# Gate terms copied raw and scaled once a batch, running totals on TensorE, z columns a step later, one subtraction a step

## The chip, the cores and the metric

The kernel runs on one core of a Trainium2 chip. Its engines run their own instruction queues in order, each queue waiting on counters of the others: TensorE (PE; its weight loads are PEld), VectorE (DVE), ScalarE (ACT), GpSimd (POOL) and SyncE (SP, which issues DMAs). The metric is the device time of one execution in microseconds; the median over several runs counts.

## The reference

The work is a linear attention, a mixture of experts on its result, and a SoLU block:

```
proj = q or k @ w_phi (64 -> 128);  proj -= max|proj|;  phi = [exp(proj), exp(-proj)]
kv = phi(k)^T v;  z = sum over tokens of phi(k)
x = (phi(q) kv) / (phi(q) z + 1e-6)                       # 8 batches x 8 heads x 576 tokens
logits = x @ w_gate + bias[modality];  expert = first argmax;  gate = softmax at it
y = gate * relu(x @ w1[expert]) @ w2[expert]              # 4608 tokens, 512 wide, 8 experts
h = y @ w_in;  solu = h * softmax(h);  out = layernorm(solu) * g_ln @ w_out
```

## The kernel before, in words

**Attention.** Eight units (a pair of batches times a half of the heads) of nine steps each make 72 steps, numbered 0 to 71. A step projects one tile of k and one of q into a PSUM tile `pj` (128x1024), from which VectorE takes the largest magnitude (`m`, L191) and subtracts it (L196, once for k into `xsk`, once for q into `xsq`). ScalarE takes the two exponentials of k (`e`, L203 and L204). Two steps later (LAGF) TensorE transposes `xsq` into a PSUM tile `tp`, of which ScalarE makes the exponentials of q (`qp`, L263), and it adds `e` into `kv` (L209); GpSimd adds `e` into `es` (L248, L224 for the remainder tiles), the sums over tokens. After the fifth and the ninth step of a unit its half is finished: ScalarE copies `kv` out (`kt`, L251), TensorE makes from it the features-to-output matrix `kf` with the gate weights folded in (L330), and, in the step after, the z columns of it from `es` by 16 matmuls of one column (`z_part`, L310 with `es`; the trace counts each twice).

**Tokens.** A token tile is 16 matmuls of `qp` by `kf` (L310, again 32 in the trace) into a `tp` tile of 73 columns a head: 64 output columns, 8 gate terms, one denominator. VectorE makes the reciprocal `r` of the denominator (L409, L410), multiplies the gate terms by it (L411, `gs`, 128x32) and the output by it (L415, `xt`, 128x256). At most two items, z columns and token tiles together, run in a step (COLS), so steps hold none, one or two token tiles; per unit there is one group of two two-token steps and a one-token step, and one group of two two-token steps. The tiles `tp` share three PSUM buffers among the transposes, `kf`, z, tokens and gating.

**Gating.** After a batch's four or five token tiles of both head halves (nine gatings in all), VectorE sums the gate terms over the heads (L427), adds the bias, finds the first largest and a one-hot `oh`. Two bf16 matmuls give the rank of a token among those of its expert in a tile and the tile's totals (L449, L450); ScalarE copies them to `g_rk` (L455), VectorE adds the totals up tile by tile in `base` (L468, L470, one small addition a tile) and computes each token's row (L475 and after), and GpSimd scatters the rows by indirect DMA (L482). From the totals, VectorE makes a table (`early.pick`, L694 to L706) by which the first chunk of expert weights is loaded, and ScalarE and VectorE split it into two parts (L776, L777) at step 63 + STEP0.

**After that** come the experts and the SoLU block, to the end of the span: float32 products made of three fp32r matmuls each. The change does not touch them.

**Order.** TensorE runs in the order in which the code is written. VectorE, ScalarE and GpSimd are put in order by a planner at build time, so an instruction's place follows from the planner's times, and a queue's head blocks all behind it.

Of the kernel before, what the change touches and what calls it, by code (L numbers as in the profile page):

```python
# [16 lines left out]
P = 128  # L17
# [3 lines left out]
E = 8  # L21
# [27 lines left out]
STEP0 = 6  # L49
# [68 lines left out]
def attention(ctx, tc, c, cnt, xe, q, qr, k, kr, v, ld, early, m, late):  # L118
# [60 lines left out]
    def project(u, jobs):  # L179
# [12 lines left out]
        return [(nm, i, features(pj[:, :, a], m[:, :, a], nm)) for a, (nm, i) in enumerate(jobs)]  # L192

    def features(pj, m, kind):
        x = w3p.tile([P, 4, F], F32, name="xs" + kind, bufs=4 if kind == "q" else 3)
        V.tensor_tensor(  # L196
            out=x.rearrange("p (j r) f -> p r j f", r=2), in0=pj,
            in1=m.unsqueeze(3).broadcast_to([P, 2, 2, F]), op=ALU.subtract,
        )
        if kind == "q":  # L200
            return x
# [134 lines left out]
    def finish_kv(u, half):  # L336
# [3 lines left out]
        after.append(Item("64", lambda: z_part(u, half), ready=lambda: step[0] > at))  # L340
# [43 lines left out]
    def tokens(u, i):  # L384
# [3 lines left out]
        if u.g == 0:  # L388
            if a == 0:
                w = 1 if part == 2 else 4  # L390
                t = xp.tile([P, w, ROW], F32, name=f"xt{w}")
# [6 lines left out]
            if i in (0, 4):  # L398
                gs[grp] = gp.tile([P, 5, H, E], F32, name="gs")
# [8 lines left out]
        r = gp.tile([P, 4], F32, name="r", bufs=3)  # L408
        V.tensor_scalar(out=r, in0=tp[:, :, D + E], scalar1=1e-6, scalar2=None, op0=ALU.add)  # L409
        V.reciprocal(r, r)  # L410
        V.tensor_tensor(  # L411
            out=gs[grp][:, i - 4 * grp, 4 * u.g : 4 * u.g + 4, :],
            in0=tp[:, :, D : D + E], in1=r.unsqueeze(2).broadcast_to([P, 4, E]), op=ALU.mult,
        )
# [5 lines left out]
    def gating(u, first, n, pace=0, counted=None):  # L420
# [3 lines left out]
        gt = gs[0][:, 0:n] if first == 0 else gs[1][:, first - 4 : first - 4 + n]  # L424
# [22 lines left out]
        rkp = tps.tile([P, 2, n, E], F32, name="tp")  # L447
        ohf = oh.rearrange("p t e -> p (t e)")
        T.matmul(rkp[:, 0].rearrange("p t e -> p (t e)"), lhsT=c.tri_bf, rhs=ohf, start=True, stop=True, skip_group_check=True)  # L449
        T.matmul(rkp[:, 1].rearrange("p t e -> p (t e)"), lhsT=c.ones_bf, rhs=ohf, start=False, stop=True, skip_group_check=True)  # L450
        rk = w("rk", [P, 2, 5, E])[:, :, :n, :]
        if tiles[0] == 7:
            V.tensor_copy(rk, rkp)
        else:
            A.copy(rk, rkp)  # L455
# [11 lines left out]
        base = w("base", [P, 6, E])  # L467
        V.tensor_copy(base[:, 0, :], cnt[0])  # L468
        for a in range(n):
# [1074 lines left out]
```

## Time and profile before

| | us |
|---|---|
| median of 3 runs | 1204.37 (1201.35 to 1208.66) |
| profiled execution: its time / its span | 1209.89 / 1207.7 |
| PE busy | 1166.4 (97 %) |
| DVE busy | 842.5 (70 %) |
| ACT busy | 576.9 (48 %) |
| POOL busy | 404.1 (33 %) |
| mean granted TensorE clock | 0.985 of full |

Attention ends at about 345 us of the span, and the experts and the SoLU block fill the rest. POOL is at six to eight tenths in attention and far below after. A share of busy time says little here: what counts is where PE, the engine that is nearly always busy, stands still, and at which clock it works after. Matmul ends are modelled, so a busy PE isn't PE at its peak.

### The profile page before, as it was taken

The page shows a single profiled execution, that of the slowest core. Times are in us where ns is not written, and L with a number is a line of the kernel's source. Part 1 is how long each engine was busy: PE and PEld are TensorE (multiplying, and loading weights), DVE is VectorE, ACT ScalarE, POOL GpSimd, SP SyncE. Part 2 cuts the span into 40 slices and gives each one's busy share as a digit, 9 for nine tenths or more (in the row PEclk, how much of TensorE's full clock was granted, in tenths as well). Part 3 has the DMA queues.
Part 4 walks back from the last instruction along what each step waited for, and adds up shares of the span by engine and source line. Part 5 has one row for each costly group of instructions (what it writes and reads, how often), then busy time and mean ns, then how long its engine had stood idle before and what let it go on. Part 6 is the DMA issues. An engine that isn't in the chain of part 4 may idle for free.

```text
span 1207.7 us, 27753 instructions
## 1 busy us (share of the span) xinstructions
PE 1166.4 (97%) x10658; PEld 1017.8 (84%) x10658; DVE 842.5 (70%) x1606; ACT 576.9 (48%) x974; POOL 404.1 (33%) x460
## 2 busy tenths in 40 slices
PE   7998999997989999999999999999999999999997
PEld 5787887886879999999999999977777778888885
DVE  6689889798666577787777877665655565566561
ACT  6455554655443455555555654643434343444342
POOL 4967867866640000000000000123233333433331
PEclk9899999999899999999999999999999999999999
DMA  9523433332231322145231324787877856556541
GB/s 322 181 80 123 137 95 120 123 122 80 86 111 62 83 86 71 53 133 166 57 85 54 88 67 129 200 206 206 226 202 202 224 136 149 147 134 151 148 119 48
DMA packets 249657, 157.40 MB, mean 130 GB/s; under 512 B 168752, under 2 KB 227376, under 8 KB 249520
## 3 DMA queue, kind: packets, MB, share of 16 engines
q1 hardware_dynamic: 243472, 136.39, 41.4%
q0 software_dynamic: 5760, 19.03, 4.1%
q8 instruction: 86, 1.41, 0.5%
q14 instruction: 51, 0.42, 0.1%
q10 hardware_dynamic: 288, 0.16, 0.0%
HBM read 167.12 MB, written 51.37 MB: 181 GB/s over the span
## 4 chain that ended last, share of the span: by engine, by line
PE 41%; DMA 6%; issue 1%; ACT 1%; DVE 1%; SPq 1%; POOLq 0%; ACTq 0%; DVEq 0%
PE tp L932 20%; PE h L932 19%; DMA turned<-whi 2%; DMA wlo<-turned 2%; DMA gd<-xe 1%; PE tp L1251 1%; SPq L1102 1%; DMA ldk<-in_moe_w_dram 1%; PE tp L747 0%; DMA gt<-gd 0%; DMA yd<-yo 0%; PE tp L1235 0%; DMA out_dram<-wab,gt 0%; ACT ex L1121 0%; ACT whi L1153 0%
## 5 line engine op out<-in xcount | busy, mean ns | idle before, releaser
L777 POOL TENSOR_TENSOR yTl<-yin,yTh 128x512 fp32r<-128x512 f32 x36 | 47.4, 1317 | 415.4 <-PE tp L932 403.1
L248 POOL TENSOR_TENSOR es<-es,e 128x512 f32<-128x512 f32 x128 | 162.1, 1273 | 50.6 <-ACT e L204 43.4
L932 PE MATMUL tp<-xTh,whi 128*128 128x256 f32 x432 | 122.1, 283 | 2.3 <-PEq L1332 2.3
L932 PE MATMUL h<-hTh,wlo 128*128 128x256 f32 x432 | 120.4, 279 | 0.8 <-DVE wlo L777 0.8
L932 PE MATMUL h<-hTl,whi 128*128 128x256 f32 x432 | 120.5, 279 | 0.4 <-DVE hTl L947 0.4
L932 PE MATMUL tp<-xTl,whi 128*128 128x256 f32 x432 | 120.9, 280 | 0.0
L932 PE MATMUL tp<-xTh,wlo 128*128 128x256 f32 x432 | 120.9, 280 | 0.0
L932 PE MATMUL h<-hTh,whi 128*128 128x256 f32 x432 | 120.3, 279 | 0.0
L191 DVE TENSOR_REDUCE m<-pj 128x8 f32<-128x1024 f32 x72 | 87.7, 1219 | 40.7 <-PE pj L186 39.8
L263 ACT ACTIVATE qp<-tp 128x512 f32<-128x512 f32 x128 | 69.1, 593 | 71.8 <-PE tp L256 68.9
L1121 ACT ACTIVATE ex<-h,s_mx,gt 128x1024 f32<-128x1024 f32 x36 | 43.5, 1208 | 124.1 <-DVE s_mx L1118 66.8
L1116 DVE TENSOR_REDUCE s_mx<-h 128x1 f32<-128x512 f32 x72 | 46.4, 686 | 78.6 <-PE h L932 78.6
L1134 POOL TENSOR_SCALAR rs<-s_var,gt 128x1 f32<-128x1 f32 x36 | 12.4, 344 | 227.1 <-ACT sq L1131 227.1
L1131 ACT ACTIVATE sq<-ex 128x1024 bf16<-128x1024 f32 x36 | 38.1, 1058 | 97.9 <-DVE ex L1128 97.9
L932 PEld LDWEIGHTS tp<-xTh,whi 128*128 128x128 f32 x432 | 81.9, 189 | 2.5 <-issue 2.4
L932 PEld LDWEIGHTS h<-hTh,wlo 128*128 128x128 f32 x432 | 81.9, 190 | 0.9 <-DVE wlo L777 0.9
L932 PEld LDWEIGHTS tp<-xTh,wlo 128*128 128x128 f32 x432 | 82.5, 191 | 0.0
L932 PEld LDWEIGHTS tp<-xTl,whi 128*128 128x128 f32 x432 | 82.0, 190 | 0.0
L932 PEld LDWEIGHTS h<-hTl,whi 128*128 128x128 f32 x432 | 81.1, 188 | 0.7 <-DVE hTl L947 0.6
L932 PEld LDWEIGHTS h<-hTh,whi 128*128 128x128 f32 x432 | 81.2, 188 | 0.0
L310 PEld LDWEIGHTS tp<-kf,qp 128*64 128x64 f32 x2048 | 70.6, 136 | 8.4 <-issue 3.1
L310 PE MATMUL tp<-kf,qp 128*64 128x73 f32 x2048 | 72.7, 227 | 2.0 <-DVE g_base L468 0.9
(377 smaller groups left out, 3384.5 us busy)
## 6 DMA issues: line engine op xcount, KB each, us to landing
ldk<-in_moe_w_dram SPq DMA_DIRECT2D x66, 512.0 KB
ldv<-in_moe_w_dram SPq DMA_DIRECT2D x66, 512.0 KB
ldq<-in_moe_w_dram SPq DMA_DIRECT2D x44, 512.0 KB
turned<-whi SPq DMA_DIRECT2D x35, 512.0 KB
wlo<-turned SPq DMA_DIRECT2D x140, 128.0 KB
yin<-yd SPq DMA_DIRECT2D x18, 512.0 KB
yd<-yo SPq DMA_DIRECT2D x35, 256.0 KB
ldv<-in_v_dram SPq DMA_DIRECT2D x16, 512.0 KB
```

The costliest lines, as they stand in the source:

```text
L191: V.tensor_reduce(out=m, in_=pj, axis=AX.X, op=ALU.max, apply_absolute_value=True)
L248: G.tensor_tensor(out=eo, in0=eo, in1=ev[:, :, r, :], op=ALU.add)
L263: A.activation(u.qp[half][:, fh, 2 * hp : 2 * hp + 2, o : o + 2 * P], tp.rearrange("p (h r) t -> p h (r t)", r=2), AF.Exp, scale=sc,)
L310: T.matmul(out(rows, h, fh), lhsT=lhsT(side, rows, h, fh), rhs=rhs(side, h, fh), start=h == 0 and fh == 0, stop=fh == 1, skip_group_check= ...
L777: eng.tensor_tensor(out=lo, in0=src, in1=hi.bitcast(F32), op=ALU.subtract)
L932: T.matmul(o, lhsT=l, rhs=r, start=first and n == 0, stop=last and n == 2, skip_group_check=True)
L1102: SP.dma_start(out=lv[g], in_=dv[g])
L1116: V.tensor_reduce(out=mx, in_=h[:, sl], axis=AX.X, op=ALU.max, negate=True)
L1121: A.activation(ex, h, AF.Exp, bias=mx, scale=g, accum_out=sm)
L1131: A.activation(sq, ex, AF.Square, accum_out=var)
L1134: G.tensor_scalar(out=rs, in0=var, scalar1=g, scalar2=g, op0=ALU.mult, op1=ALU.mult)
L1251: T.matmul(b[group(g), dh, :], lhsT=ht[fh][:, f, group(g)], rhs=m.w1c(j % 2 * NMINI + g)[:, f, :], start=j == f == 0, stop=fh == 1 and f = ...
```

## The change

Five edits. The gate terms go to SBUF unscaled by a ScalarE copy for each token tile, `r` is kept for the whole batch, and one GpSimd multiplication a gating applies it. The running totals are made by TensorE: the single matmul with ones becomes one for each tile of the gating, accumulating in the same PSUM tile, so that two VectorE additions of the old total replace the copy and the chain of `base`; the table is made there, one yield earlier. The z columns are made a step later, save in the last unit and one other place. The two subtractions of a step become one of 128x1024, and the exponentials of k start after it. The first chunk of weights is split two steps later. Token buffers `xt1` go from three to two.

```diff
-STEP0 = 6
+STEP0 = 8
@@ project
-        return [(nm, i, features(pj[:, :, a], m[:, :, a], nm)) for a, (nm, i) in enumerate(jobs)]
-
-    def features(pj, m, kind):
-        x = w3p.tile([P, 4, F], F32, name="xs" + kind, bufs=4 if kind == "q" else 3)
+        x = w3p.tile([P, 8, F], F32, name="xs", bufs=4)
         V.tensor_tensor(
-            out=x.rearrange("p (j r) f -> p r j f", r=2), in0=pj,
-            in1=m.unsqueeze(3).broadcast_to([P, 2, 2, F]), op=ALU.subtract,
+            out=x.rearrange("p (aj r) f -> p r aj f", r=2), in0=pj.rearrange("p r a j f -> p r (a j) f"),
+            in1=m.rearrange("p r a j -> p r (a j)").unsqueeze(3).broadcast_to([P, 2, 4, F]), op=ALU.subtract,
         )
+        xs = [x[:, 4 * a : 4 * a + 4] for a in range(2)]
+        return [(nm, i, keys(x) if nm == "k" else x) for (nm, i), x in zip(jobs, xs)]
@@ finish_kv
-        after.append(Item("64", lambda: z_part(u, half), ready=lambda: step[0] > at))
+        soon = u is last_unit() or u.p2 == 2 and u.g == half == 1
+        after.append(Item("64", lambda: z_part(u, half), ready=lambda: step[0] > at + (not soon)))
@@ tokens
-                gs[grp] = gp.tile([P, 5, H, E], F32, name="gs")
+                gs[grp] = gp.tile([P, 5, H, E], F32, name="gs"), gp.tile([P, 5, H], F32, name="gr")
-        r = gp.tile([P, 4], F32, name="r", bufs=3)
+        at = (slice(None), i - 4 * grp, slice(4 * u.g, 4 * u.g + 4))
+        r = gs[grp][1][at]
+        A.copy(gs[grp][0][at], tp[:, :, D : D + E])
         V.tensor_scalar(out=r, in0=tp[:, :, D + E], scalar1=1e-6, scalar2=None, op0=ALU.add)
         V.reciprocal(r, r)
-        V.tensor_tensor(
-            out=gs[grp][:, i - 4 * grp, 4 * u.g : 4 * u.g + 4, :],
-            in0=tp[:, :, D : D + E], in1=r.unsqueeze(2).broadcast_to([P, 4, E]), op=ALU.mult,
-        )
@@ gating
+        G.tensor_tensor(out=gt, in0=gt, in1=r.unsqueeze(3).broadcast_to([P, n, H, E]), op=ALU.mult)
@@ gating, after the one-hot
-        T.matmul(rkp[:, 1].rearrange("p t e -> p (t e)"), lhsT=c.ones_bf, rhs=ohf, start=False, stop=True, skip_group_check=True)
-        rk = w("rk", [P, 2, 5, E])[:, :, :n, :]
-        if tiles[0] == 7:
-            V.tensor_copy(rk, rkp)
-        else:
-            A.copy(rk, rkp)
+        for a in range(n):
+            T.matmul(
+                rkp[:, a + 1 : n + 1], lhsT=c.ones_bf, rhs=oh[:, a : a + 1].broadcast_to([P, n - a, E]),
+                start=False, stop=True, skip_group_check=True,
+            )
+        old, cnt[0] = cnt[0], w("cnt", [P, E])
+        V.tensor_tensor(out=cnt[0], in0=rkp[:, n], in1=old, op=ALU.add)
+        rkb = w("rkb")[:, :n, :]
+        V.tensor_tensor(out=rkb, in0=rkp[:, 0:n], in1=old.unsqueeze(1).broadcast_to([P, n, E]), op=ALU.add)
+        if counted:
+            counted()
@@ gating, after the yield
-        base = w("base", [P, 6, E])
-        V.tensor_copy(base[:, 0, :], cnt[0])
-        for a in range(n):
-            V.tensor_tensor(out=base[:, a + 1, :], in0=rk[:, 1, a, :], in1=base[:, a, :], op=ALU.add)
-        cnt[0] = base[:, n, :]
-        if counted:
-            counted()
-        rkb = w("rkb")[:, :n, :]
-        V.tensor_tensor(out=rkb, in0=rk[:, 0], in1=base[:, :n, :], op=ALU.add)
```

The instructions of three places, before and after. First VectorE in a step with two token tiles, with the engines that each row waits for; before:

```order
L191 TENSOR_REDUCE m<-pj 128x8 [waits PE_49]
L196 TENSOR_TENSOR xsk<-pj,m 128x2x2x128 [waits DVE_49,Activation_49]
L196 TENSOR_TENSOR xsq<-pj,m 128x2x2x128
L409 TENSOR_SCALAR r<-tp 128x4 [waits PE_49]
L410 RECIPROCAL r<-r 128x4 [waits DVE_49]
L411 TENSOR_TENSOR gs<-tp,r 128x32 [waits DVE_49]
L415 TENSOR_TENSOR xt_772<-tp,r 128x256
L191 TENSOR_REDUCE m<-pj 128x8 [waits PE_49]
```

And of the changed kernel, where `gr` is the tile that keeps `r`, both token tiles:

```order
L191 TENSOR_REDUCE m<-pj 128x8 [waits PE_49]
L193 TENSOR_TENSOR xs<-pj,m 128x2x4x128 [waits DVE_49]
L411 TENSOR_SCALAR gr<-tp 128x4 [waits Activation_49]
L412 RECIPROCAL gr<-gr 128x4 [waits DVE_49]
L413 TENSOR_TENSOR xt_509<-tp,gr 128x256 [waits DVE_49]
L411 TENSOR_SCALAR gr<-tp 128x4 [waits Activation_49]
L412 RECIPROCAL gr<-gr 128x4 [waits DVE_49]
L413 TENSOR_TENSOR xt_509<-tp,gr 128x256 [waits DVE_49]
L191 TENSOR_REDUCE m<-pj 128x8 [waits PE_49]
```

The first operation on a token tile waited for TensorE and now waits for ScalarE, which copies the gate terms of the same tile.

Second ScalarE in steps with token tiles; before:

```order
L263 ACTIVATE qp<-tp 128x2x256 [waits PE_49]
L263 ACTIVATE qp<-tp 128x2x256
L203 ACTIVATE e<-xsk 128x4x128 [waits DVE_49,Activation_49,Pool_49]
L204 ACTIVATE e<-xsk 128x4x128
L263 ACTIVATE qp<-tp 128x2x256 [waits PE_49]
L263 ACTIVATE qp<-tp 128x2x256
```

And of the changed kernel:

```order
L262 ACTIVATE qp<-tp 128x2x256 [waits PE_49]
L262 ACTIVATE qp<-tp 128x2x256
L202 ACTIVATE e<-xs 128x4x128 [waits DVE_49,Activation_49,Pool_49]
L203 ACTIVATE e<-xs 128x4x128
L410 COPY gs<-tp 128x32 [waits PE_49] x2
L262 ACTIVATE qp<-tp 128x2x256 [waits PE_49]
L262 ACTIVATE qp<-tp 128x2x256
```

The two copies of the gate terms stand behind the exponentials of k of the same step, which wait for VectorE.

Third TensorE around the z columns of a first half (`used` with `es` is z, `used` with `kt` is `kf`); before:

```order
L330 MATMUL tp<-used,kt 128x144 x4
L209 MATMUL kv<-e,ldrv 64x256 x4
L209 MATMUL kv<-e,ldv 64x256 x4
L310 MATMUL tp<-used,es 64x1 x16
L186 MATMUL pj<-wphi,ldk 128x128 x4
```

And of the changed kernel:

```order
L329 MATMUL tp<-used,kt 128x144 x4
L208 MATMUL kv<-e,ldrv 64x256 x4
L208 MATMUL kv<-e,ldv 64x256 x4
L186 MATMUL pj<-wphi,ldk 128x128 x4
L186 MATMUL pj<-wphi,ldq 128x128 x4
L255 MATMUL tp<-kept,xs 128x128 x4
L208 MATMUL kv<-e,ldv 64x256 x4
L309 MATMUL tp<-used,es 64x1 x16
```

One whole step of projection, transposes and `kv` stands ahead of the z columns now.

## Rows read from the trace of the kernel before

**Rows 1.** Windows: length; PE, PEld, DVE, ACT, POOL busy; PEclk, DMA share, GB/s.

```profile
80.58:163.08 82.50, 78.97 (x1261) 64.12 (x1262) 73.45 (x165) 44.84 (x92) 63.39 (x59) 0.98 0.37 117
141.68:146.40 4.72, 4.72 (x93) 4.06 (x94) 4.24 (x11) 2.24 (x4) 4.56 (x4) 1.00 0.20 59
150.11:152.80 2.69, 2.69 (x29) 1.86 (x30) 2.52 (x4) 2.12 (x5) 2.54 (x2) 1.00 0.36 125
420.00:1207.00 787.00, 776.25 (x5106) 690.63 (x5105) 515.65 (x786) 364.65 (x562) 146.31 (x216) 1.00 0.50 134
```

**Rows 2.** Timeline, a two-token step: start, length, engine, line; idle before.

```profile
141.68 1.23 DVE L191 TENSOR_REDUCE m<-pj 128x8 f32<-128x1024 f32 x1
...
143.06 2.20 PE L310 MATMUL tp<-kf,qp 128*64 128x73 f32 x64
143.62 0.68 DVE L196 TENSOR_TENSOR xsq<-pj,m 128x512 f32<-128x512 f32 x1
143.80 0.63 ACT L203 ACTIVATE e<-xsk 128x512 f32<-128x512 f32 x1 [0.45 <-DVE xsk L196]
...
144.33 0.61 ACT L204 ACTIVATE e<-xsk 128x512 f32<-128x512 f32 x1
...
146.87 1.08 PE L209 MATMUL kv<-e,ldv 128*64 128x256 f32 x8
```

**Rows 3.** Timeline, one token on VectorE at its own pace.

```profile
292.32 0.15 DVE L409 TENSOR_SCALAR r<-tp 128x4 f32<-128x4 f32 x1
...
292.72 0.19 DVE L411 TENSOR_TENSOR gs<-tp,r 128x32 f32<-128x32 f32 x1
...
293.16 1.22 DVE L191 TENSOR_REDUCE m<-pj 128x8 f32<-128x1024 f32 x1
```

**Rows 4.** Groups by line, 40 to 360 us: busy, mean ns, idle before.

```profile
L186 PEld LDWEIGHTS pj<-wphi,ldk 64*128 64x128 f32 x448 | 29.6, 189 | 7.4 <-issue 2.7 <-DVE g_L L428 1.2 <-DVE xt L415 0.4
...
L470 DVE TENSOR_TENSOR g_base<-g_rk,g_base 128x8 f32<-128x8 f32 x36 | 20.4, 565 | 0.5
...
L324 ACT COPY kf<-tp 128x8 f32<-128x8 f32 x15 | 2.5, 166 | 7.9 <-PE tp L310 7.9
```

**Rows 5.** Timeline, z columns of the third unit, what holds them.

```profile
110.45 2.35 POOL L224 TENSOR_TENSOR es<-es,e 64x1024 f32<-64x1024 f32 x1 [2.39 <-DMA xe<-xt,g_dsti]
110.57 2.29 DVE L431 TENSOR_TENSOR g_L<-g_L,g_mx 128x40 f32<-128x40 f32 x1
...
113.08 3.86 POOL L248 TENSOR_TENSOR es<-es,e 128x512 f32<-128x512 f32 x3
...
115.78 1.10 PE L310 MATMUL tp<-used,es 128*64 128x1 f32 x32 [2.31 <-POOL es L248]
```

**Rows 6.** Timeline, z columns of the fifth unit.

```profile
197.57 1.10 PE L310 MATMUL tp<-used,es 128*64 128x1 f32 x32 [1.59 <-issue]
```

**Rows 7.** Timeline, z columns of the seventh unit.

```profile
278.47 1.10 PE L310 MATMUL tp<-used,es 128*64 128x1 f32 x32 [1.36 <-issue]
```

**Rows 8.** Windows behind four waits of TensorE; the clock is PEclk.

```profile
117.00:121.00 4.00, 4.00 (x30) 3.03 (x30) 3.84 (x7) 2.72 (x7) 3.32 (x5) 0.57 0.57 176
199.00:203.00 4.00, 4.00 (x36) 2.99 (x35) 2.85 (x4) 2.55 (x8) 3.60 (x4) 0.57 0.62 195
281.00:285.00 4.00, 4.00 (x89) 3.58 (x89) 3.93 (x5) 2.36 (x5) 4.00 (x4) 1.00 0.02 4
298.00:309.00 11.00, 10.21 (x80) 8.08 (x81) 6.48 (x9) 6.00 (x14) 5.97 (x5) 0.53 0.24 77
```

**Rows 9.** Timeline, start of the program, first z columns.

```profile
32.81 1.88 PE L310 MATMUL tp<-used,es 128*64 128x1 f32 x32 [4.85 <-POOL es L224]
...
35.26 0.68 POOL L109 TENSOR_TENSOR bias<-msk,mb 128x288 f32<-128x288 f32 x1
```

**Rows 10.** Timeline, first weight chunk, the wait behind it.

```profile
296.23 1.04 ACT L776 CAST w<-ldk 128x1024 fp32r<-128x1024 f32 x1 [4.00 <-DMA ldk<-in_moe_w_dram]
...
298.79 2.29 PE L330 MATMUL tp<-used,kt 128*128 128x144 f32 x8 [4.46 <-ACT kt L251]
```

More of the change, by code (lines that the diff above doesn't have):

```diff
@@ L191, in project, with keys @@
         V.tensor_reduce(out=m, in_=pj, axis=AX.X, op=ALU.max, apply_absolute_value=True)
-        return [(nm, i, features(pj[:, :, a], m[:, :, a], nm)) for a, (nm, i) in enumerate(jobs)]
-    def features(pj, m, kind):
-        x = w3p.tile([P, 4, F], F32, name="xs" + kind, bufs=4 if kind == "q" else 3)
+        x = w3p.tile([P, 8, F], F32, name="xs", bufs=4)
         V.tensor_tensor(
-            out=x.rearrange("p (j r) f -> p r j f", r=2), in0=pj,
-            in1=m.unsqueeze(3).broadcast_to([P, 2, 2, F]), op=ALU.subtract,
-        )
-        if kind == "q":
-            return x
+            out=x.rearrange("p (aj r) f -> p r aj f", r=2), in0=pj.rearrange("p r a j f -> p r (a j) f"),
+            in1=m.rearrange("p r a j -> p r (a j)").unsqueeze(3).broadcast_to([P, 2, 4, F]), op=ALU.subtract,
+        )
+        xs = [x[:, 4 * a : 4 * a + 4] for a in range(2)]
+        return [(nm, i, keys(x) if nm == "k" else x) for (nm, i), x in zip(jobs, xs)]
+    def keys(x):
         e = w3p.tile([P, 4, 2, F], F32, name="e", bufs=4)
@@ L390, in tokens @@
                 w = 1 if part == 2 else 4
-                t = xp.tile([P, w, ROW], F32, name=f"xt{w}")
+                t = xp.tile([P, w, ROW], F32, name=f"xt{w}", bufs=3 if w == 4 else 2)
                 t0 = 9 * u.p2 + i
@@ L423, in gating @@
         t0 = 9 * u.p2 + first
-        gt = gs[0][:, 0:n] if first == 0 else gs[1][:, first - 4 : first - 4 + n]
+        gt, r = [t[:, 0:n] if first == 0 else t[:, first - 4 : first - 4 + n] for t in gs[first > 0]]
+        G.tensor_tensor(out=gt, in0=gt, in1=r.unsqueeze(3).broadcast_to([P, n, H, E]), op=ALU.mult)
         w = lambda nm, sh=[P, 5, E], dt=F32: gp.tile(sh, dt, name="g_" + nm)
@@ L446, in gating @@
         yield "f", 2
-        rkp = tps.tile([P, 2, n, E], F32, name="tp")
-        ohf = oh.rearrange("p t e -> p (t e)")
-        T.matmul(rkp[:, 0].rearrange("p t e -> p (t e)"), lhsT=c.tri_bf, rhs=ohf, start=True, stop=True, skip_group_check=True)
-        T.matmul(rkp[:, 1].rearrange("p t e -> p (t e)"), lhsT=c.ones_bf, rhs=ohf, start=False, stop=True, skip_group_check=True)
-        rk = w("rk", [P, 2, 5, E])[:, :, :n, :]
-        if tiles[0] == 7:
-            V.tensor_copy(rk, rkp)
-        else:
-            A.copy(rk, rkp)
+        rkp = tps.tile([P, n + 1, E], F32, name="tp")
+        T.matmul(
+            rkp[:, 0:n].rearrange("p t e -> p (t e)"), lhsT=c.tri_bf, rhs=oh.rearrange("p t e -> p (t e)"),
+            start=True, stop=True, skip_group_check=True,
+        )
+        for a in range(n):
+            T.matmul(
+                rkp[:, a + 1 : n + 1], lhsT=c.ones_bf, rhs=oh[:, a : a + 1].broadcast_to([P, n - a, E]),
+                start=False, stop=True, skip_group_check=True,
+            )
+        old, cnt[0] = cnt[0], w("cnt", [P, E])
[4 more added lines that the diff above has]
+            counted()
         sm = w("sm", [P, 5])[:, :n]
@@ L505, in first_rows @@
             T.transpose(tp[:, j, :], m.x0[:, j * P : (j + 1) * P], c.ident)
-        m.x0T = w3p.tile([P, 4, P], F32, name="xsk")
+        m.x0T = w3p.tile([P, 8, P], F32, name="xs", bufs=4)[:, 0:4]
         A.copy(m.x0T, tp)
```

## The prediction, made before the changed kernel ran

> **What bounds the kernel now.** I read the windows by stage first [rows 1]. From 420 us on, after attention, TensorE (PE) is busy 776.25 of 787.0 us at full clock, and the change touches nothing there. All it can win or lose lies in the first 345 us. In one full cycle of attention (two units, 18 steps) PE is busy 78.97 of 82.5 us at a granted clock of 0.98: it bounds this stage too, and only its pauses, and the slow clock after some of them, can be won. Next I looked for these pauses in the timeline, and at each for what ended it. The largest are the z columns: they wait for GpSimd's sums `es`, 4.85 us at the start [rows 9] and then 2.31, 1.59 and 1.36 us, once in each cycle [rows 5 to 7]. The fourth kind is a single wait of 4.46 us of the `kf` matmuls for ScalarE's copy `kt`, which stood behind a cast that waited 4.00 us for the first weight chunk [rows 10]. The windows behind them show the clock [rows 8]: after the waits of 2.31 and 1.59 us it is 0.57 over 4 us, one stretch at 1.2 instead of 2.4 GHz, which costs 4.0 x 0.43 = 1.7 us each; after the 4.46 us it is 0.53 over 11 us, 5.2 us lost; after the wait of 1.36 us it stays at 1.00. Last I read a step with two token tiles [rows 1, 2]: PE fills all 4.72 us of it, VectorE 4.24. So VectorE is the next in line, with little room.
>
> **The change, part by part.**
>
> *z a step later.* A step without token tiles holds 2.69 us of PE work [rows 1], and this stands ahead of z now. It covers all three waits inside attention (the longest is 2.31), so 2.31 + 1.59 + 1.36 = 5.3 us go, and with the first two their slow clock, 2 x 1.7 = 3.4. Of the cover 2.69 - 2.31 = 0.4 us is left, and if GpSimd comes later than that, z waits again. At the start the order on GpSimd puts two bias operations of 0.68 [rows 9] ahead of the `es` additions, so z waits 4.85 + 1.36 - 2.69 = 3.5 instead of 4.85: 1.4 gained, and the slow clock behind it remains.
>
> *Gate terms through ScalarE.* VectorE gives up 72 multiplications of 0.19 [rows 3], ScalarE takes 72 copies; the nearest row is a PSUM copy of 128x8 at 0.166 [rows 4], a 128x512 exponential takes 0.63 at the other end [rows 2], and I take 0.17, since 32 columns are near 8. ScalarE has the time. But the order ties a knot: VectorE's first operation on a token tile now waits for this copy, the copy stands behind the two exponentials of k, and these wait for VectorE's subtraction of the same step. Queued behind the waiting operation are both token tiles and the next step's maximum, for which the next subtraction and so PE's transposes and `kv` wait. Its parts that are in rows [rows 2, 3]: both exponentials, 143.80 to 144.94 = 1.14, and the token tiles. A tile with its multiplication took 292.32 to 293.16 = 0.84, of which L411 accounts for between 0.11 (start to start of what follows) and 0.19; I take 0.70 without it, 1.40 for two.
>
> *One subtraction.* From the maximum's start to the end of the second half 141.68 to 144.30 = 2.62 us pass [rows 2]. One subtraction of 128x1024 is not in the trace; the maximum over as much takes 1.23, and two of these in a row are 2.46, while no gain at all leaves 2.62. I take 2.53, near the middle. The hop to the exponentials I put at 0.10 (the first began 0.18 after the q half had, so it is hardly more). Their start so moves from 143.80 to 141.68 + 2.53 + 0.10 = 144.31, by 0.5.
>
> Loop: 2.53 + 0.10 + 1.14 + copy and hop 0.17 + 0.10 + 1.40 = 5.44 us against PE's 4.72, so a two-token step falls 0.72 back; with one token tile it is 4.74 against 4.72 - 1.10 = 3.62 [rows 2], 1.1 back. In steps without token tiles VectorE's 2.52 less 0.1 against PE's 2.69 [rows 1] gives some 0.3 a step back. The cover: `kv` starts at 146.87, its `e` was there at 144.94, 1.9 us earlier, less the 0.5 of the later exponentials, 1.4. Two two-token steps fall 1.44 back: nothing lost. With the one-token step behind them it is 2.54, so PE loses 1.1; if the late token tiles also keep all three PSUM buffers at the `kf` matmuls that follow, I estimate 1.9, with nothing lost as the other end (should the copies slip in ahead). Between 40 and 290 us there are six such groups: 6 x 1.1 = 6.6 us lost, bounds 0 and 11.4.
>
> *Totals on TensorE.* VectorE gives up 36 additions of 0.565 mean [rows 4]; that mean is high because many stall: a VectorE operation on a 128x40 tile took 2.29 us while GpSimd's addition beside it took 2.35 [rows 5]. PE waited 1.2 us in all for such a VectorE operation before projections [rows 4]; the bias addition and its neighbour stay, so I take half, 0.6 gained, bounds 0 and 1.2. PE gets 27 more matmuls; 64 with their weight loads took 2.20 us [rows 2], 0.034 each, so 0.9 us.
>
> The Trainium skill ("GPSIMD Engine Reference", Specifications) says that GpSimd's SBUF interface is shared with VectorE and contended by VectorE instructions with two SBUF inputs; the pair in [rows 5] agrees, 2.29 beside 2.35. The new additions read PSUM on one side and would be free of it, but by the same rule the new multiplication on GpSimd is one more op that holds VectorE up, which would take back that 0.6.
>
> *The multiplication on GpSimd.* 128x512 additions take 3.86 / 3 = 1.29 [rows 5], so by size 128x256 is 0.64 (from 0.2, as for a small VectorE operation, to 1.29). VectorE's sum over the heads waits for it, and the step's subtraction is queued behind. GpSimd is busy 63.39 of 82.5 [rows 1]; beside the chain of gating, which has steps of room, it costs nothing, except at the last gatings.
>
> *First weights.* The cast still stands between the same two pairs of exponentials, only `kt` has moved ahead of it. So `kf` no longer waits, but the copies of gate terms behind the cast do, with them the token tiles and their PSUM buffers, and PE stops one step later. The work between shortens the 4.46 by some 0.6; bounds 0, and 4.46 with the 5.2 of clock.
>
> *The end of attention.* The last gatings are on the path: +0.27 for copy and hop and +0.64, less the chain of totals (3 to 5 additions of 0.565 [rows 4], or of 0.15 as the shortest operation of [rows 3]): -1.9 to +0.5. The last unit does both pairs of k exponentials in one step, 1.14 more ahead of the copies. I take +1.0, bounds -2 and +2.
>
> **Sum**, against the profiled execution's own 1209.89 us: -1.4 - 5.3 - 3.4 - 0.6 + 6.6 + 0.9 - 0.6 + 1.0 = -2.8, so 1207.1. That execution lies 5.5 above the median of the runs; on the median, 1204.37 - 2.8 = 1201.6 us. The largest gain and the largest loss are of one size, and I forecast no change that can be told (under 0.5%, 6 us, is not told from none here).
>
> **The rivals.**
>
> *VectorE's relief reaches PE.* The buffers cover the loop, or the planned order lets the tiles through, and the 6.6 are not lost: 1201.6 - 6.6 = 1195.0; with PE's other pauses, 82.5 - 78.97 - 2.31 = 1.2 in each of three cycles, gone too, about 1191. For it: VectorE gives up 72 x 0.19 = 13.7 us and the 20.4 of the small additions [rows 4]; PE's own work in a cycle is only 78.97. Against: the loop passes through three engines in every token step.
>
> *The wait for the first weights vanishes* with its slow clock: 4.46 + 5.2 - 0.6 = 9.1 more, 1192.5. For it: `kt` stands free. Against: the token tiles behind the cast need the same three buffers.
>
> *Slower: the token loop becomes PE's new wait, and brings the slow clock.* Place: the `kf` matmuls behind each group of three token steps, where PE waits for a PSUM buffer. At 1.9 us each it costs 6 x 0.8 = 4.8 more, and as the wait of 1.59 was followed by a slow stretch and that of 1.36 was not [rows 6 to 8], from some 1.5 us on each brings 1.7: 10.2. That is 1201.6 + 15.0 = 1216.6; the deciding point is a wait of about 1.5. For it: my estimate of the wait lies on either side of that point. Against: the groups may be broken up, since a later z takes a place among the two items of a step.
>
> *The change doesn't do what it says:* z still waits, as GpSimd's additions come a step later as well. For the first cycle 0.4 us would suffice; I give it 0.03, and about 1207.
>
> **How the numbers follow.** No change to tell of, 1201.6 with its own range 1196 to 1208: 0.42. Relief: 0.22. Weights: 0.12. Slower loop: 0.21. z still waits: 0.03. Faster by over 0.5% (below 1198.4) is most of the relief and weight cases and a quarter of the first: 0.20 + 0.11 + 0.11 = 0.42. Slower (above 1210.4) is the loop's case with 0.2 and a little of the others: 0.22. The rest, 0.36, is no change. The range goes from 1190 to 1214: it leaves out half of the slower case and a little of the faster ones.
>
> **What would show it.** In the changed profile PE's waits at the z columns inside attention should be gone and the clock at 1.00 behind them. A step with two token tiles should take about 5.4 us from one maximum to the next where PE isn't waited for, with VectorE waiting for ScalarE's copy; and behind six groups PE should wait about 1 us at a `kf` or a transpose. If VectorE's first token operation hardly waits, the relief is right. If those waits are near 2 us with clocks of 0.57 after them, the slower rival is. One 4-us wait with a slow stretch of about 10 us near 295 us should still be there; if not, the weights' rival holds.

## The result, and the profile after

The changed kernel takes 1219.2 us (median of 4 runs, 1216.72 to 1225.16) against 1204.05 for the kernel before on the same chip: a ratio of 1.0129, 95% interval 1.0102 to 1.0157. Forecast was no change, 1201.6; the time lies above the range. Its profiled execution took 1219.56 us with a span of 1217.8, against 1209.89 and 1207.7: 10.1 us longer. The first expert matmul starts at 375.1 us of the span instead of 360.4, so attention alone is 14.7 us longer, about what the medians differ by; the part behind it, which no edit touches, came out 4.6 us shorter in this one execution.

First the windows (columns as in [rows 1]): one cycle of 18 steps, a step with two token tiles, two stretches of slow clock, and the part after attention.

```profile
77.00:163.68 86.68, 80.30 (x1268) 64.40 (x1269) 63.60 (x121) 46.33 (x109) 64.75 (x60) 0.98 0.34 111
140.70:146.05 5.35, 5.35 (x98) 4.52 (x100) 3.80 (x8) 2.69 (x9) 5.12 (x6) 1.00 0.25 75
113.00:117.00 4.00, 4.00 (x30) 2.78 (x28) 0.79 (x2) 0.00 (x0) 4.00 (x4) 0.60 0.39 76
211.00:215.00 4.00, 4.00 (x72) 3.86 (x67) 3.46 (x10) 1.88 (x5) 3.31 (x4) 0.60 0.02 4
...
420.00:1217.00 797.00, 787.80 (x5216) 703.22 (x5214) 524.54 (x800) 371.90 (x572) 147.14 (x216) 1.00 0.50 135
```

A cycle takes 86.68 us instead of 82.50, although VectorE is busy 63.60 instead of 73.45: it gave up ten microseconds of work and the cycle grew by four. The two-token step takes 5.35 us instead of 4.72. The waits say where the time goes (engine, instruction, what it waited for, us in total, times, longest; 40 to 370 us):

```profile
DVE gr L411 <- ACT gs L410: 49.0, 34, 4.1
...
ACT e L202 <- DVE g_L L427: 18.5, 5, 6.3
DVE g_L L426 <- POOL gs L423: 14.1, 8, 4.5
...
PE tp L309 <- ACT kf L323: 9.6, 5, 2.9
...
ACT e L202 <- POOL es L216: 6.9, 3, 3.0
...
PE tp L329 <- ACT qp L262: 5.9, 5, 1.2
```

The first line is the loop that the prediction worked out: VectorE waits for ScalarE's copies. The third is the multiplication on GpSimd, which the prediction priced at nothing inside attention. The fourth and last are TensorE's own new waits, 9.6 and 5.9 us. The z waits inside attention [rows 5 to 7] are gone. In the timeline, a two-token step:

```profile
146.05 1.21 DVE L191 TENSOR_REDUCE m<-pj 128x8 f32<-128x1024 f32 x1
...
147.30 1.23 DVE L193 TENSOR_TENSOR xs<-pj,m 128x1024 f32<-128x1024 f32 x1
148.64 0.63 ACT L202 ACTIVATE e<-xs 128x512 f32<-128x512 f32 x1 [1.55 <-DVE xs L193]
...
149.69 0.26 ACT L410 COPY gs<-tp 128x32 f32<-128x32 f32 x2
149.90 0.16 DVE L411 TENSOR_SCALAR gr<-tp 128x4 f32<-128x4 f32 x1 [1.37 <-ACT gs L410]
...
151.38 1.22 DVE L191 TENSOR_REDUCE m<-pj 128x8 f32<-128x1024 f32 x1
```

Maximum, subtraction, exponentials, copies, token tiles, and again: VectorE stands 1.37 us in this turn, as in most. The next lines are from the third unit, the place where z waited before [rows 5]:

```profile
109.01 2.35 POOL L223 TENSOR_TENSOR es<-es,e 64x1024 f32<-64x1024 f32 x1 [2.20 <-DMA xe<-xt,g_dsti]
...
115.44 0.74 POOL L423 TENSOR_TENSOR gs<-gs,gr 128x320 f32<-128x320 f32 x1
...
116.21 0.74 DVE L426 TENSOR_REDUCE g_L<-gs 128x40 f32<-128x320 f32 x1 [4.54 <-POOL gs L423]
...
116.87 1.21 DVE L193 TENSOR_TENSOR xs<-pj,m 128x1024 f32<-128x1024 f32 x1
...
117.52 1.05 PE L309 MATMUL tp<-used,es 128*64 128x1 f32 x32
...
118.20 0.63 ACT L202 ACTIVATE e<-xs 128x512 f32<-128x512 f32 x1 [6.35 <-DVE g_L L427]
...
123.42 0.63 ACT L202 ACTIVATE e<-xs 128x512 f32<-128x512 f32 x1 [2.97 <-POOL es L216]
...
124.47 0.15 ACT L323 COPY kf<-tp 128x8 f32<-128x8 f32 x1
...
124.68 2.25 PE L309 MATMUL tp<-kf,qp 128*64 128x73 f32 x64 [2.88 <-ACT kf L323]
```

Read it from the top. GpSimd comes late, as before. The multiplication stands behind its additions, VectorE's sum waits 4.54 us for it with the step's subtraction behind, and ScalarE's exponentials wait for that. The z matmuls at 117.52 no longer wait. But their result must be copied by ScalarE (L323), the copy stands behind a pair of exponentials that waits for GpSimd once more (its fill of the next `es`, L216), and the token tiles wait 2.88 us for the copy. The wait left the z columns and came back one instruction further on.

Standstills of TensorE up to the first expert matmul (stretches of over 0.1 us with no PE and no PEld instruction, us), by what ended them, and what the slow clock cost up to there (time at less than the full granted clock, times the share that was lacking). "z es" are the z columns waiting for `es`, "z copy" the token tiles waiting for the copied z, "qp,gs" ScalarE's exponentials of q and copies of gate terms, "weights" the one wait beside the first weight chunk; "none" are standstills for which neither the matmul nor its weight load shows anything that ended a wait, called standstills without a releaser from here on. Each row is one execution.

```
                          z es  z copy  qp,gs  VectorE  none  weights  other  all   slow clock
before                    12.5    -      -       4.7     -      4.5     1.0   22.7    12.3
changed                    3.4   9.6    7.3      7.0     -      4.8     1.2   33.3    13.7
totals, late z only        1.2   0.2     -       6.1    3.5     4.7     1.2   16.9     6.8
the same, scatter later    3.1   0.4     -       5.2     -      4.7     1.4   14.7     6.8
```

9.1 us of z waits went, 9.6 came back at the copy, and 9.6 came at ScalarE and VectorE. With 1.4 us more of slow clock that is 12 of the 14.7; besides, TensorE is busy longer, 80.30 against 78.97 us in a cycle [rows 1], and what makes it so is not shown. The expectations below go by the weight load's row alone. That gives 1.0 us without a releaser for the kernel before and 10.9 for the first run; by the matmul's own row 1.0 and 2.1 of these were waits for VectorE.

### The profile page after: what moved, and what is told of

Read it like the earlier page. It is cut to its first block, busy times and chain, and to the rows that moved or that the text cites. A ratio compares the mean times of both kernels' runs of the same rounds, so it can differ in the third digit from the quotient of the medians.

```text
span 1217.8 us, 27667 instructions
## 1 busy us (share of the span) xinstructions
PE 1167.6 (96%) x10685; PEld 1017.6 (84%) x10685; DVE 813.7 (67%) x1425; ACT 582.3 (48%) x1038; POOL 410.3 (34%) x469
## 4 chain that ended last, share of the span: by engine, by line
PE 46%; DMA 2%; issue 1%; ACT 1%; SPq 0%; DVE 0%; POOLq 0%; ACTq 0%; DVEq 0%
PE tp L929 22%; PE h L929 22%; DMA turned<-whi 1%; PE tp L1232 1%; PE tp L1248 1%; DMA wlo<-turned 1%; PE tp L744 0%; SPq L1099 0%; DMA out_dram<-wab,gt 0%; ACT ex L1118 0%; DVE ex L1123 0%; ACT wab L1160 0%; POOLq L1537 0%; ACT whi L1150 0%; ACT whi L773 0%
## 5 line engine op out<-in xcount | busy, mean ns | idle before, releaser
L202 ACT ACTIVATE e<-xs 128x512 f32<-128x512 f32 x72 | 45.3, 630 | 107.1 <-DVE xs L193 61.1
L193 DVE TENSOR_TENSOR xs<-pj,m 128x1024 f32<-128x1024 f32 x72 | 88.0, 1223 | 2.4
L309 PEld LDWEIGHTS tp<-kf,qp 128*64 128x64 f32 x2048 | 73.4, 142 | 16.4 <-ACT kf L323 9.9
L309 PE MATMUL tp<-kf,qp 128*64 128x73 f32 x2048 | 75.9, 233 | 9.3 <-ACT kf L323 8.6
```

What stands on the lines that cost most here:

```text
L193: V.tensor_tensor(out=x.rearrange("p (aj r) f -> p r aj f", r=2), in0=pj.rearrange("p r a j f -> p r (a j) f"), in1=m.rearrange("p r a j - ...
L309: T.matmul(out(rows, h, fh), lhsT=lhsT(side, rows, h, fh), rhs=rhs(side, h, fh), start=h == 0 and fh == 0, stop=fh == 1, skip_group_check= ...
```

## The experiments

Each kernel is compared with the kernel before on the same chip; ratios stand with 95% intervals. The chips differ (the kernel before takes 1204 to 1212 us), so ratios say how much an edit is worth, and the traces, one execution each, say where TensorE stood. Diffs are cut to the lines that matter, and `...` stands for what is left out of a line. First, the gate part undone in the changed kernel, and done alone in the kernel before.

**Gate terms by VectorE again, the rest of the change kept.**

```diff
-        A.copy(gs[grp][0][at], tp[:, :, D : D + E])
+        V.tensor_tensor(out=gs[grp][0][at], in0=tp[:, :, D : D + E], in1=r..., op=ALU.mult)
-        G.tensor_tensor(out=gt, in0=gt, in1=r..., op=ALU.mult)
```

> The changed kernel with its gate terms scaled by VectorE tile by tile, as before the change; the other four edits stay. Theory: the whole loss, and more, comes from the gate terms' way over ScalarE and GpSimd. Then both new waits go (VectorE for ScalarE's copy, 49.0 us in all in the changed kernel, and VectorE for GpSimd's multiplication, 14.1 us), a step with two token tiles takes 4.7 us instead of 5.34, and with the z waits gone as well the time is about 1196 us (1190 to 1201), below the kernel before. Rival: the single subtraction and the later z columns cost as much by themselves; then 1206 to 1215.

Measured: 0.9961 (0.9946 to 0.9976), 1207.21 against 1211.44 us. The whole loss of the change goes with the gate part. By the ratio the time is near the upper edge of what was expected; what still holds it up is taken up below.

**The gate part alone, on the kernel before.**

```diff
-        V.tensor_tensor(out=gs[grp][:, i - 4 * grp, ...], in0=tp[:, :, D : D + E], in1=r..., op=ALU.mult)
+        A.copy(gs[grp][0][at], tp[:, :, D : D + E])
+        G.tensor_tensor(out=gt, in0=gt, in1=r..., op=ALU.mult)      # in gating
```

> The kernel before with the gate part alone: copies by ScalarE, multiplication by GpSimd; two subtractions, totals on VectorE and z columns as before. Theory: the gate part loses what the other edits cannot give back: 1204 + 15 to 30, so 1219 to 1234, as here the z waits stay and VectorE has the chain of totals besides. Rival, that the loss needs the single subtraction with it: 1203 to 1212.

Measured: 1.0000 (0.9984 to 1.0016). The rival was right in this: alone the gate part costs nothing that can be told. The two-token step of this run:

```profile
138.56 1.23 DVE L191 TENSOR_REDUCE m<-pj 128x8 f32<-128x1024 f32 x1 [1.55 <-PE pj L186]
...
140.62 0.63 ACT L203 ACTIVATE e<-xsk 128x512 f32<-128x512 f32 x1 [0.40 <-DVE xsk L196]
...
141.88 0.16 DVE L411 TENSOR_SCALAR gr<-tp 128x4 f32<-128x4 f32 x1 [0.78 <-ACT gs L410]
...
143.37 1.22 DVE L191 TENSOR_REDUCE m<-pj 128x8 f32<-128x1024 f32 x1
```

With two subtractions the exponentials start 2.06 us after the maximum; with one it is 2.59 (146.05 to 148.64). The loop takes 4.81 us, 0.1 above TensorE's 4.72, where the changed kernel's takes 5.35.

**The two together on the kernel before**: the edit above, and this.

```diff
-        x = w3p.tile([P, 4, F], F32, name="xs" + kind, bufs=4 if kind == "q" else 3)
+        x = w3p.tile([P, 8, F], F32, name="xs", bufs=4)      # one subtraction for k and q
```

With the single subtraction the token buffer `xt1` also goes from three to two, here and wherever it is done on the kernel before.

> The kernel before with the gate part and the single subtraction, nothing else (z columns, totals and first weights as before). Theory: these two together make the loss: two-token steps of 5.34 us, ratio to the kernel before 1.008 to 1.016. Rival, that the later z or the totals are needed for the loss: 0.998 to 1.004.

Measured: 1.0177 (1.0157 to 1.0196). As the theory had it, somewhat more: these two make a larger loss, 21 us by the ratio, than the whole change does. The waits behind token steps are not where most of it lies. TensorE waits 2.0 us in all for `qp`, but stands 8.7 us without a releaser, where the kernel before never does, and the slow clock costs 23.9 us up to the first expert matmul instead of 12.3. 8.5 of these lie in stretches that begin in or just behind a group of such standstills, as here at those of 225 to 229 and 290 to 293 us (windows, columns as in [rows 1]):

```profile
227.00:235.00 8.00, 6.75 (x39) 4.58 (x40) 3.98 (x8) 2.45 (x7) 5.45 (x9) 0.57 0.23 89
292.00:300.00 8.00, 6.93 (x63) 5.46 (x63) 3.98 (x8) 2.69 (x7) 7.19 (x7) 0.57 0.16 51
```

**Two subtractions in the changed kernel.**

```diff
-        x = w3p.tile([P, 8, F], F32, name="xs", bufs=4)      # one subtraction for k and q
+        return [(nm, i, features(pj[:, :, a], m[:, :, a], nm)) for a, (nm, i) in enumerate(jobs)]
```

> The changed kernel with two subtractions a step as before; gate terms by ScalarE and GpSimd, totals on TensorE, later z stay. Theory (loop plus subtraction): the exponentials of k start some 0.5 us earlier, a two-token step takes 4.80 us instead of 5.34, the waits of 1.15 us behind three token steps go; the copy's loop alone was free of loss in the run with the gate part on the kernel before. Ratio to the kernel before 0.995 to 1.005, if the waits of 2.8 us at the z copies shrink as well, since everything before them is earlier; 1.005 to 1.010 if they stay. Rival, that later z columns or the totals bring the loss: 1.011 to 1.016 as the changed kernel.

Measured: 1.0075 (1.0051 to 1.0098). The waits of 1.15 us behind three token steps are gone, and half of the loss stays. Projections now wait for VectorE's subtraction, which stands behind the wait for the multiplication (waits, 40 to 300 us):

```profile
DVE g_L L427 <- POOL gs L424: 17.4, 6, 5.9
PE pj L186 <- DVE xsq L196: 6.4, 3, 2.5
```

TensorE also stands 5.2 us without a releaser. This kernel differs from the one with totals and late z alone (0.9879, below) by the gate part only. So beside those two the gate part costs 2.0 %, although the loop has its short form here, with two subtractions.

**The multiplication on VectorE**, in that kernel and in the changed one.

```diff
-        G.tensor_tensor(out=gt, in0=gt, in1=r..., op=ALU.mult)
+        V.tensor_tensor(out=gt, in0=gt, in1=r..., op=ALU.mult)
```

> The changed kernel with two subtractions a step (1.0075) and, besides, the batch's multiplication of gate terms on VectorE instead of GpSimd. Theory: of the loss left with two subtractions the multiplication's wait in GpSimd's queue is the larger part (projections waited 6.3 us for VectorE's subtraction, which stood behind that wait, and slow clocks followed): these waits go, ratio 0.994 to 1.002. Rival, that the copies by ScalarE make what is left: 1.005 to 1.010.

Measured: 1.0037 (1.0023 to 1.0051), between theory and rival. The waits for the subtraction are gone, but as much came at other operations of VectorE (11.7 us in all, 11.8 without the edit), and those at the z copy grew from 3.9 to 7.3 us. What fell are the standstills without a releaser, 5.2 to 0.1 us, and the slow clock, 17.1 to 12.0. So the 0.4 % can't be put down to the multiplication's wait alone.

> The changed kernel with the multiplication of a batch's gate terms on VectorE instead of GpSimd; the copies by ScalarE stay. Theory: of the loss the multiplication's place in GpSimd's queue is one part: VectorE's sum over the heads then waits no more (4.5 us at 116 us of the span), the three waits of TensorE of 2.8 to 2.9 us behind it go with the slow clock around them, 3 x (2.9 + 0.3) + 2 to 4 = about 12 us: 1207 (1203 to 1212), while two-token steps stay at 5.34 us. Rival, that the loop of the copies makes the whole loss: 1217 to 1220.

Measured: 1.0178 (1.0155 to 1.0201), outside both. The waits at the z copy stayed at 8.7 us, so beside the single subtraction they don't come from the multiplication alone, and TensorE stood still 8.1 us without a releaser, where the changed kernel never does.

**ScalarE's copy written behind VectorE's operations**, so that ScalarE waits and not VectorE.

```diff
-        A.copy(gs[grp][0][at], tp[:, :, D : D + E])
         V.tensor_scalar(out=r, ...)
         V.reciprocal(r, r)
         V.tensor_tensor(out=xs[part]..., op=ALU.mult)
+        A.copy(gs[grp][0][at], tp[:, :, D : D + E])
```

> The changed kernel with ScalarE's copy of the gate terms written behind VectorE's three operations on the same token tile, so that ScalarE waits for VectorE and not VectorE for ScalarE; the multiplication on GpSimd stays. Theory of two parts: the loop is cut, two-token steps take 4.7 instead of 5.34 us, the waits of TensorE of 1.15 us behind three token steps (five of them) go and some of the slow clock, the waits of 2.9 us stay: 1208 (1204 to 1213). Rival, that the loop is the whole loss: 1196 to 1201. Rival, that the loop only uses up slack: 1216 to 1220.

Measured: 1.0091 (1.0070 to 1.0112). The loop is cut and TensorE's waits of 1.15 us for `qp` are gone (1.6 us left of 6.6, 0.6 of them before 300 us), but the z copy still costs 9.1, and 8.1 us of standstills without a releaser came. The loop is at most a part of the loss, not the whole.

**The z columns at their old step, in the changed kernel.**

```diff
-ready=lambda: step[0] > at + (not soon)
+ready=lambda: step[0] > at
```

> The changed kernel with its z columns in the step after the half, as before; the rest of the change stays. Theory: the later z is worth its three waits at GpSimd's sums, some 5 us and two slow stretches, and costs the three waits of 2.8 us of token tiles for ScalarE's copy of the z columns; about even: ratio to the kernel before 1.008 to 1.016. Rival, that the copy of the late z columns, stuck behind exponentials, is a large part of the loss: 1.000 to 1.006.

Measured: 1.0198 (1.0164 to 1.0233), worse than expected. Late z is worth about 0.7 %, some 8 us, in the changed kernel, even with the wait that came in its place. Beside the run with the gate part and the single subtraction (1.0177) this kernel has the totals on TensorE and the later first weights: with the early z they gain nothing.

**The z copy by VectorE, in the changed kernel.**

```diff
-        A.copy(u.kf[half][:, :, :, D + E : HW], tp.unsqueeze(3))
+        V.tensor_copy(u.kf[half][:, :, :, D + E : HW], tp.unsqueeze(3))
```

> The changed kernel with the copy of the z columns out of PSUM on VectorE instead of ScalarE, nothing else. Theory: token tiles wait for this copy (9.5 us in all, three times 2.8 to 2.9) because it stands on ScalarE behind the exponentials of k, which wait for GpSimd; on VectorE it stands behind a subtraction, and the three waits fall to under 0.5 us each: 7 to 9 us and some slow clock less, ratio 1.002 to 1.008. Rival, that the wait is GpSimd's lateness and only moves on: 1.010 to 1.015.

Measured: 1.0104 (1.0087 to 1.0121). The waits fell from 9.6 to 2.1 us, nearly as the theory said of them (one of the three is left at 1.6); the time did not follow. The waits for `qp` and `gs` grew by 3.1 us and the slow clock by 3.4. The rival was right: the lateness moves on.

Then the other edits apart.

**The late z alone, on the kernel before.**

```diff
-STEP0 = 6
+STEP0 = 8
-ready=lambda: step[0] > at
+ready=lambda: step[0] > at + (not soon)
```

> The kernel before with the later z columns (and the first weights split two steps later) alone; totals on VectorE, two subtractions, gate terms by VectorE. Theory: the later z is the larger part of what the run with z and totals gained (0.988): z waits inside attention gone with their slow clock, ratio 0.990 to 0.996. Rival, that the totals on TensorE carry that gain: 0.997 to 1.003.

Measured: 1.0011 (0.9995 to 1.0027). The rival was right: without the totals on TensorE the late z gains nothing. The timeline shows why; the chain of totals now falls beside GpSimd's additions:

```profile
95.71 4.80 POOL L224 TENSOR_TENSOR es<-es,e 64x1024 f32<-64x1024 f32 x2
...
95.89 2.21 DVE L471 TENSOR_TENSOR g_base<-g_rk,g_base 128x8 f32<-128x8 f32 x1
...
98.22 2.34 DVE L476 TENSOR_TENSOR g_rkb<-g_rk,g_base 128x32 f32<-128x32 f32 x1
...
101.14 1.07 PE L310 MATMUL tp<-kf,qp 128*64 128x73 f32 x27 [2.84 <-DVE g_base L469]
```

Two small additions of SBUF tiles take as long as the two operations of GpSimd beside them, and the token tiles wait 2.84 us for VectorE. In the changed kernel their successors, which read PSUM, take 0.156 (128x8) and 0.18 us on the mean. In all TensorE waits 17.0 us for VectorE here, 6.1 with the totals on TensorE.

**The single subtraction alone, on the kernel before** (the diff of the run with the two together, without the gate part).

> The kernel before with the single subtraction alone. Theory: without the copies nothing waits for the later exponentials, and PE fills its steps; ratio to the kernel before 0.998 to 1.004. Rival, from the pair of runs without copies (0.996 with one subtraction, 0.988 with two): the single subtraction costs by itself, 1.005 to 1.010, and the trace has TensorE standing still without a releaser inside token tiles, more than the 1.0 us of the kernel before.

Measured: 1.0083 (1.0050 to 1.0115), the rival's number and its sign: 9.3 us without a releaser. The two `xt1` buffers are not told apart from it here; but the pair at 0.996 and 0.988, which has two of them both times, gives the same 0.8 %.

**Totals and late z, with two subtractions and gate terms by VectorE** (the first run's diff and that of two subtractions, on the changed kernel).

> The changed kernel with gate terms scaled by VectorE and two subtractions a step: what is left of the change is the totals on TensorE, the later z and the later first weights. Theory: without the copies the subtraction is hidden, so ratio 0.993 to 0.999, as with one subtraction (0.996). Rival, that the single subtraction gains by itself: 0.999 to 1.004. In the run with one subtraction TensorE stood still for want of instructions (gaps of 0.3 to 0.6 us) in token tiles during the scatter of rows; if that hangs on where the scatter falls, the gaps change here.

Measured: 0.9879 (0.9861 to 0.9898), lower than the theory's range. Two cycles of it:

```profile
72.20:150.66 78.46, 77.38 (x1268) 63.68 (x1269) 68.06 (x157) 44.77 (x90) 63.27 (x59) 1.00 0.38 124
150.66:235.50 84.84, 82.10 (x1268) 66.18 (x1269) 69.89 (x156) 44.82 (x90) 63.17 (x59) 0.96 0.36 114
```

The first is nearly what TensorE needs, 78.46 us at full clock. The second is 6.4 longer, mainly for one group of standstills without a releaser, 2.2 us at 198 to 203 us, and a slow clock behind it that costs 3.4.

**First weights split at step 73 instead of 71** in that kernel (`STEP0 = 10` for `STEP0 = 8`).

> Totals on TensorE and later z, with two subtractions and gate terms by VectorE (the run at 0.988), and the first weights split four steps later than before the change instead of two. The cast by ScalarE then stands two steps later than the chunk's arrival. Theory: TensorE's wait of 4.7 us for the copy behind the cast goes, and the slow clock of 3.4 us behind it: ratio 0.980 to 0.985. Rival, that the wait only moves: 0.986 to 0.990.

Measured: 0.9883 (0.9861 to 0.9905). The wait stayed (4.4 us): the rival was right.

**The scatter asked for one step later**, with one subtraction and with two.

```diff
-        yield "0", 1
+        yield "0", 2
```

> The changed kernel with gate terms by VectorE (one subtraction; 0.996) with the scatter of rows and the sums ahead of it asked for one step later. Theory: TensorE's standstills without a releaser (10.9 us in the run without this edit, at 99 to 101 and 124 to 128 us of the span) come from its instructions arriving late while the scatter's transfers fill the DMA engines in steps with two token tiles. Here the second scatter of a batch falls behind those steps; then the gaps near 124 to 128 go, the total falls to 4 to 7 us and the ratio to 0.988 to 0.993. Rival, that they hang on the place in the program and not on the scatter: the gaps stay, 0.995 to 0.998.

Measured: 0.9924 (0.9906 to 0.9941), as the theory said. Without the edit, TensorE's matmuls and the scatter's transfers stand like this (timeline):

```profile
122.46 0.97 POOL L480 DMA_INDIRECT xe<-xt,g_dsti  x1 [0.30 <-issue]
...
122.87 1.43 PE L309 MATMUL tp<-kf,qp 128*64 128x73 f32 x38
...
123.74 0.96 POOL L480 DMA_INDIRECT xe<-xt,g_dsti  x1 [0.30 <-issue]
124.65 0.41 PE L309 MATMUL tp<-kf,qp 128*64 128x73 f32 x6 [0.35 <-issue]
...
125.38 0.38 PE L309 MATMUL tp<-kf,qp 128*64 128x73 f32 x5 [0.32 <-issue]
...
126.81 0.36 PE L309 MATMUL tp<-kf,qp 128*64 128x73 f32 x4 [1.05 <-issue]
...
128.23 0.60 PE L309 MATMUL tp<-kf,qp 128*64 128x73 f32 x11 [1.07 <-issue]
```

Two token tiles that take 2.20 us [rows 2] take 5.96 here: after every five matmuls or so TensorE stands, waiting for nothing that the profile shows, while rows are scattered. With the edit the same tiles run ahead of the scatter:

```profile
120.33 2.20 PE L309 MATMUL tp<-kf,qp 128*64 128x73 f32 x64
122.17 1.02 POOL L480 DMA_INDIRECT xe<-xt,g_dsti  x1 [1.26 <-DVE gr L411]
```

The standstills without a releaser fell from 8.9 to 4.9 us, and two slow stretches of 1.7 us, after them at 102 and 129 us, are gone. The second edit is on the kernel with two subtractions.

> Totals on TensorE and later z, two subtractions, gate terms by VectorE (0.988), with the scatter asked for one step later as in the run that took it from 0.996 to 0.992. Theory: TensorE's standstills without a releaser (5.9 us, and a slow stretch of 3.4) halve again: ratio 0.982 to 0.986. Rival: 0.987 to 0.990, if the scatter finds other steps with two token tiles.

Measured: 0.9870 (0.9853 to 0.9886), 1189.83 against 1205.44 us. The 3.5 us of standstills without a releaser are gone, but z waits 1.9 us longer, the slow clock up to the first expert matmul costs the same 6.8, and the ratio is not told apart from that of the run without the edit: the rival's band. It is the lowest of all, 1.3 % below the kernel before.

## Why the prediction was wrong

*The step that failed* is the price of the gate part with the single subtraction: "6 x 1.1 = 6.6 us lost, bounds 0 and 11.4." Done on the kernel before with nothing else, the two cost 1.77 %, 21 us. Taken out of the changed kernel they give back more still, 1.0129 to 0.9879. The other terms of the sum come to -9.4 us; by the runs they are -6 beside the two and -15 without them, so the 18 us of the miss lie mainly in this one. The step counted the loop's own waits, and these came as forecast. It put at nothing what the loop does elsewhere: the standstills without a releaser (8.7 us in the run with the two, none before) and the slow clock (23.9 us instead of 12.3), which the sum left out and only the slower rival had a price for. In the changed kernel TensorE stands at the z copy and for VectorE instead, and never without a releaser.

*Right:* the loop's length. Forecast 5.44 us against 4.72, measured 5.35; forecast 1.1 us lost behind each of six groups, measured 1.14 to 1.16 behind five. The copies took 0.18 each (0.17 counted), the subtraction 1.23, 1.25 after the maximum's start. What the prediction lacked is that the two edits weigh on each other and on the rest: gate part alone 1.000, single subtraction alone 1.008, both 1.018; and beside totals and late z the gate part costs 2.0 % even with two subtractions. It treated the two as one term and so could not see that either might be dropped.

*A second step that failed:* "It covers all three waits inside attention (the longest is 2.31), so 2.31 + 1.59 + 1.36 = 5.3 us go, and with the first two their slow clock". The z matmuls did stop waiting. But the step asked only when `es` is ready, not when the result is used. The token tiles of the next step need z copied, and the copy stood on ScalarE behind exponentials that wait for the same late GpSimd. Three waits of 2.82 to 2.88 us and two of 0.49 came, 9.6 us, more than the 5.3, and the slow clock cost 1.4 us more where 3.4 less were counted. This failed only together with the gate part. In the kernels with late z that have the gate terms by VectorE, 0.4 us or less is left at the copy; and measured by undoing it, late z is worth some 8 us in the changed kernel too, near the 8.7 that the sum gave it.

*The third that failed:* the multiplication "beside the chain of gating, which has steps of room, it costs nothing". Its length was right (0.63 for 128x256 against 0.64 by size), but what stands ahead of it on GpSimd was not counted: VectorE waited 14.1 us for it, 11.9 of them in three waits, one in each cycle. The queue was named and then priced by its mean load, 63.39 of 82.5. Moving it to VectorE gained 0.4 % with two subtractions, not by its own wait alone; with one it made no gain.

*Totals on TensorE* were priced at 0.6 us gained against 0.9 lost. With late z they are worth more: 0.988 with them, 1.001 without, with TensorE waiting 6.1 and 17.0 us for VectorE and the slow clock at 6.8 and 13.7. The prediction had the rows for it [rows 4, 5], but priced only the waits already there, not those that a later z would bring. Totals alone were not run.

*The start:* the changed kernel is 3.6 us ahead at step 18, where 1.4 were counted: z waited 3.12 and not 3.5, and the slow stretch behind it cost 1.7 instead of 3.4. *First weights:* still a wait of 4.81 us, the bound of no gain; the slow stretch behind it cost 3.4 instead of 5.1. *The end of attention:* from the last maximum to the first expert matmul 30.9 us, before 31.0; 1.0 had been added.

*The slower rival* gave 1216.6 and the sign; its mechanism was only half there, and that the time lies so near 1219.2 is luck. The groups' waits stayed at 1.15 instead of 1.9 us, and its deciding point did not hold: the slow stretch at 112 to 117 us followed a wait of 1.16, while the four other waits of that length, and one of 1.36 before [rows 7, 8], were followed by none. The length of a wait alone doesn't tell when the clock falls.

*The relief rival* was right about VectorE's room: with the gate part and the single subtraction left out, the first of two cycles takes 78.46 us, near the 77.38 that TensorE is busy in it.

*What stays open:* by which way the gate part costs what it does. Cutting the loop, moving the multiplication and moving the z copy each took away its own wait and left most of the time, or all of it. Nor is it shown how the z copy's waits hang on ScalarE's copies of gate terms. They come with late z and those copies, 3.9 to 9.6 us in five kernels, with the multiplication on either engine, and not with late z alone. How much of each ratio is the place of the scatter is open too, as the runs differ in both.

## What to carry to other kernels

When work moves to another engine, ask what stands ahead of it in that engine's queue and whether that waits for the engine relieved: here three engines in turn made a loop that no busy share shows. When a wait is hidden at one instruction, follow its result to the next user before counting the gain. And test parts of a bundle in pairs, each beside the others: two edits that cost nothing and 0.8 % alone cost 1.8 % together, the one that cost nothing alone costs 2.0 % beside the rest of the bundle, and that rest gave 1.2 % once both were out.

## What the runs showed that was not expected

TensorE can stand still without any wait in the profile. While GpSimd's row scatter runs, a stretch of 64 token matmuls that takes 2.20 us elsewhere took 5.96, in pieces of about five matmuls with 0.3 to 0.6 us between; such standstills, nearly all beside a scatter, sum to 8.9 us in the first run above and to 9.3 in the run with the single subtraction alone, against none in the kernel before. Moving the scatter by one step removed 4.0 us of the 8.9, and all 3.5 in the kernel with two subtractions. So the scatter's place matters; but a scatter beside a token tile is not enough, as the kernel before shows, where the tile goes through:

```profile
125.01 1.02 POOL L482 DMA_INDIRECT xe<-xt,g_dsti  x1 [1.29 <-DVE r L410]
...
125.72 2.24 PE L310 MATMUL tp<-kf,qp 128*64 128x73 f32 x64
...
126.33 0.97 POOL L482 DMA_INDIRECT xe<-xt,g_dsti  x1 [0.30 <-issue]
```

The DMA share is 0.46 there (126 to 129 us) and 0.91 in the standing stretch (124 to 129 us of the first run). What holds TensorE is open. That its instructions arrive late, as one expectation has it, is inferred from the missing releaser alone; the trace doesn't bear it out, as none of the DMA packets of that stretch (121.5 to 129 us) is an instruction packet. The single subtraction alone cost 0.8 % with 9.3 us of these standstills in its trace. That they are its price is likely, not shown: its z waits fell by 6.1 us besides, and its slow clock rose by 3.1.
